# Splitting the first matmul of chunk 0 so that a part of it runs inside the attention that comes before it

## The chip, the cores and the metric

The kernel runs on one core of a Trainium2 chip. The metric is the device time of one execution in microseconds; the median over several executions is quoted, and a trace of one execution shows where the time goes. Every trace counts from its own first instruction, and where that zero lies differs from trace to trace by about 1 us. So intervals inside one trace are compared here, and absolute times only with that in mind.

## The reference, cut to what matters

```python
# q, k, v: (8 rows, 8 heads, 576 positions, 64)
# heads 0..3: sliding window of 32; heads 4..7: every fourth position of a window of 128
attn = softmax(mask(q @ k.T / 8)) @ v                # per row and head
x = attn.transpose(0, 2, 1, 3).reshape(8 * 576, 512) # 4608 tokens
h = x @ w_in                                         # 512 -> 2048  ("mm1")
g = relu(h) ** 2
out = g @ w_out                                      # 2048 -> 512  ("mm2")
```

The 4608 tokens go through mm1 and mm2 in nine chunks of 512. Chunk 0 is the first 512 of row 0's 576 tokens, so it needs all of row 0's attention; its mm2 runs interleaved with the attention of row 1.

## The kernel before: the parts that matter

One ff tile of mm1 is four matmuls (one for each 128 of the 512 features) into a PSUM bank, then a relu on ScalarE and, for each pair of tiles, a square on VectorE:

```python
def mm1_gen(c, g, sm=None):
    xs = xT[:, :, c * TOKC : (c + 1) * TOKC]
    for ffc in range(NFF):                           # 16 ff tiles
        ph = pmool.tile([P, TOKC], FP32, ...)
        for n, dmk in enumerate((2, 3, 0, 1)):
            nc.tensor.matmul(ph, wi[:, dmk, ffc * P : ffc * P + P], xs[:, dmk, :], ...)
            if n == 1:
                yield
        relu_squared(c, ffc, g, ph, rts)
        yield
```

`pump(n)` takes n steps of the pending generator, which is how matmuls are laid between other work. The end of row 0's attention, the loads for row 1, and chunk 0:

```python
    zs = av_dilated(0, 1, 0)
    s_sliding_half(1, 1)
    x_dilated(0, 0, ys, False)
    idle(4)                                  # zero matmuls: keep TensorE's clock up
    zs += av_dilated(0, 1, 1)
    xs += av_sliding(0, 3, 5)
    xs += av_sliding(0, 5, 6, nc.scalar)
    constants_late()
    idle(16)
    x_dilated(0, 1, zs, False)               # transposes, then a ScalarE copy into xT
    idle(16)
    x_sliding(0, 1, xs, False)
    idle(12)

    load_w_out(0, 1)                         # GpSimd's queue
    landed(wi[:, NDM - 1, 1023:1024])        # GpSimd waits for w_in's second quarter
    nc.gpsimd.memset(sq[:, :, :, 0:1], 0.0)
    load_sliding_qk(1)                       # sq: row 1's sliding q and k (SyncE's queue)
    load_dilated_qk(1)                       # nd_: row 1's dilated q and k
    load_w_out(1, 2)
    landed(nd_[:, 0, 1, 12 * D - 1 :])
    ...                                      # memsets
    load_v(1)
    landed(sv[:, NB - 1, HH - 1, D - 1 :])
    load_w_out(2, 4)
    dk = keep_qk(2)

    g0 = hidden(0)
    pending.append(mm1_gen(0, g0))
    pump(28)                                 # 14 of 16 tiles
    cast_sliding_qk(1, (nc.scalar, nc.vector, nc.scalar, nc.vector))   # reads sq
    pump(1000)
    pending.append(mm2_by_rows_gen(0, g0))
    pump(1)
    for hp in range(2):
        for i in (1, 0):
            t_sliding(1, hp, i, True)        # transposes of the casts
            pump(1)                          # two matmuls of mm2
    ...
```

The softmax here doesn't subtract the row's maximum and nothing guards it: scores larger than these inputs give would overflow.

## Time and profile before

| | |
|---|---|
| time, first three executions | 306.88 us median (306.87 to 307.14) |
| TensorE busy | 296.3 of 305.5 us |
| zero matmuls in the second half of row 0's attention (16.9 to 25.0 us) | 60 |
| chunk 0's mm1, undivided | 13.97 us, from 24.96 to 38.93 (13.81 of it, from 25.12, on the chain that ends last) |
| first transposes of row 1 | 39.21 us |
| chunk 1's mm1 starts | 63.25 us |

How to read it: TensorE is the resource, but "busy" counts zeros too. The lines that carry this are in the prediction and not shown again. A granted clock of 1.00 means TensorE at full speed. Names in the lines: ph and po are the PSUM tiles of mm1 and mm2, rt is a tile after the relu, sq holds row 1's sliding q and k as loaded, early their casts to 16 bits, pt the transposes of those and QKTp the copy of pt.

### The profile page before, as it was taken

The numbers are of one execution on the slowest core, as the hardware profiler recorded it, in microseconds if no ns is written. First come the engines' busy times: TensorE is split into PE (matmuls) and PEld (weight loads), VectorE is DVE, ScalarE is ACT, GpSimd is POOL, SyncE is SP. The second block draws the span as 40 slices with busy tenths as digits, with TensorE's granted clock in tenths as the row PEclk, the third lists the DMA queues.
The fourth block names the chain that finished last, engine by engine and source line by source line (L and its number), as shares of the span: only waits on it lengthen the run. The fifth ranks groups of instructions, "written<-read, shape, count | busy, mean of one in ns | idle before, by whom it ended". The sixth has DMA issues, their size and how long they took to land.

```text
span 305.5 us, 7013 instructions
## 1 busy us (share of the span) xinstructions
PE 296.3 (97%) x2898; PEld 192.8 (63%) x2898; DVE 208.8 (68%) x410; ACT 185.0 (61%) x308; POOL 48.5 (16%) x97
## 2 busy tenths in 40 slices
PE   8899998999999999999999999999999999999994
PEld 3675444444696469646964697459745974684584
DVE  4653475849966797679766977697769775843744
ACT  6466777478834893489348943894389437405610
POOL 7454013006004100320032003200100010000000
PEclk9999999999999999999999999999999999999999
DMA  8999989899899998689939983989310012003004
GB/s 175 226 213 230 233 174 203 160 232 269 210 191 219 310 170 185 217 182 198 228 111 197 216 184 123 213 184 209 117 72 0 2 61 78 2 0 137 2 0 138
DMA packets 85615, 47.89 MB, mean 157 GB/s; under 512 B 68112, under 2 KB 82896, under 8 KB 85200
## 3 DMA queue, kind: packets, MB, share of 16 engines
q1 hardware_dynamic: 76688, 27.24, 40.8%
q0 software_dynamic: 8352, 19.80, 28.9%
q8 instruction: 22, 0.36, 0.5%
q10 hardware_dynamic: 544, 0.43, 0.5%
q14 instruction: 9, 0.07, 0.1%
HBM read 39.85 MB, written 16.52 MB: 184 GB/s over the span
## 4 chain that ended last, share of the span: by engine, by line
PE 90%; ACT 3%; DMA 3%; POOL 2%; issue 1%; DVE 1%; ACTq 0%; POOLq 0%
PE ph L388 42%; PE pob L438 9%; PE poa L438 9%; PE poe L438 5%; PE poc L438 5%; PE pod L438 4%; PE po L409 4%; DMA early<-in_q_dram 3%; PE paw L776 3%; PE pav L759 2%; PE pz L675 2%; PE ps L656 1%; PE py L809 1%; PE px L791 1%; POOL early L119 1%; ACT AT L628 1%
## 5 line engine op out<-in xcount | busy, mean ns | idle before, releaser
L388 PE MATMUL ph<-xT,wi 128*128 128x512 f16 x576 | 129.8, 379 | 0.0
L354 ACT ACTIVATE rt<-ph 128x512 f16<-128x512 f32 x144 | 84.9, 601 | 36.4 <-PE ph L388 36.1
L388 PEld LDWEIGHTS <-wi 128*128 128x128 f16 x576 | 54.4, 98 | 62.4
L358 DVE TENSOR_TENSOR g<-rt 128x1024 f16<-128x1024 f16 x63 | 43.5, 691 | 47.2 <-ACT rt L354 47.0
L438 PEld LDWEIGHTS <-sm 128*128 128x128 f16 x512 | 46.9, 98 | 4.8
L438 PEld LDWEIGHTS <-g 128*128 128x128 f16 x384 | 35.9, 98 | 6.9 <-DVE g L356 1.3
L438 PE MATMUL pob<-T,sm 128*128 128x256 f16 x256 | 32.5, 272 | 0.0
L438 PE MATMUL poa<-wo,g 128*128 128x256 f16 x256 | 32.4, 273 | 0.0
L458 POOL DMA_DIRECT2D out_dram<-otl x6 | 4.6, 763 | 152.6 <-DVE otl L493 152.6
L815 ACT COPY xT<-py 128x576 f16<-128x576 f16 x16 | 10.2, 640 | 27.3 <-PE py L809 27.3
L740 DVE TENSOR_TENSOR x_d<-paw,rcp_d 72x512 f16<-72x512 f32 x32 | 22.0, 687 | 1.1
L797 ACT COPY xT<-px 128x576 f16<-128x576 f16 x16 | 10.3, 642 | 13.6 <-PE px L791 13.6
L409 PE MATMUL po<-wo,g 128*128 128x512 f16 x64 | 17.8, 379 | 0.0
L735 DVE RECIPROCAL rcp_d<-paw 72x8 f32<-72x8 f32 x32 | 6.4, 199 | 16.2 <-PE paw L776 16.2
L628 ACT ACTIVATE AT<-pz 128x576 f16<-128x576 f32 x28 | 16.6, 652 | 1.0 <-PE pz L675 0.6
L628 ACT ACTIVATE AT<-ps 128x576 f16<-128x576 f32 x28 | 16.6, 649 | 0.5
L740 DVE TENSOR_TENSOR x_p<-pav,rcp_p 96x512 f16<-96x512 f32 (+1 forms) x24 | 16.2, 676 | 0.8
L438 PE MATMUL poe<-wo,sm 128*128 128x256 f16 x128 | 16.3, 273 | 0.0
L438 PE MATMUL pod<-T,g 128*128 128x256 f16 x128 | 16.3, 272 | 0.0
L438 PE MATMUL poc<-T,sm 128*128 128x256 f16 x128 | 16.2, 272 | 0.0
L478 ACT COPY otu<-poa 128x512 f32<-128x512 f32 x8 | 4.7, 586 | 17.5 <-PE poa L438 17.5
L629 DVE TENSOR_TENSOR AT<-AT,maskd 128x576 f16<-128x576 f16 x28 | 12.2, 455 | 3.5 <-ACT AT L628 2.5
(120 smaller groups left out, 354.5 us busy)
## 6 DMA issues: line engine op xcount, KB each, us to landing
sv<-in_v_dram SPq DMA_DIRECT2D x40, 128.0 KB, 3.1
sd<-in_v_dram SPq DMA_DIRECT2D x8, 512.0 KB, 6.2
dk<-in_k_dram POOLq DMA_DIRECT2D x12, 288.0 KB, 7.0
dk<-in_q_dram POOLq DMA_DIRECT2D x12, 288.0 KB, 7.5
out_dram<-otl POOLq DMA_DIRECT2D x6, 512.0 KB, 3.3
out_dram<-otu POOLq DMA_DIRECT2D x6, 512.0 KB, 4.2
sd<-in_v_dram SPq DMA_DIRECT2D x8, 288.0 KB
wi<-in_moe_w_in_dram POOLq DMA_DIRECT2D x4, 512.0 KB, 10.3
```

The source lines that it names most:

```text
L354: nc.scalar.activation(rt[:, o, :], ph[:], ACTF.Relu)
L358: nc.vector.tensor_mul(g[:, ffc - 1 : ffc + 1, :], rt, rt)
L388: nc.tensor.matmul(ph, wi[:, dmk, ffc * P : ffc * P + P], xs[:, dmk, :], start=(n == 0), stop=(n == NDM - 1),)
L409: nc.tensor.matmul(po, g[:, ffc, t * P : (t + 1) * P], wo[:, ffc, :], start=(ffc == 0), stop=(ffc == NFF - 1),)
L438: nc.tensor.matmul(acc, lhs[:, k, t * P : (t + 1) * P], rhs[:, k, :], start=(first and k == 0), stop=(k == NK - 1), skip_group_check=True,)
L628: nc.scalar.activation(AT[:, u, 0:UW], ps[:, :, 0 : UW // 2], ACTF.Exp, scale=scale)
L629: nc.vector.tensor_mul(AT[:, u, 0:UW], AT[:, u, 0:UW], mask)
L735: nc.vector.reciprocal(rcp[0:w, 0:n], pv[:, :, :, D])
L740: nc.vector.tensor_tensor(out=x[0:w, 0:n], in0=pv[:, :, :, 0:D], in1=rcp[0:w, 0:n].unsqueeze(3).to_broadcast([w, n, HH, D]), op=ALU.mult,)
L776: nc.tensor.matmul(pav[:, e, h * (D + 2) : h * (D + 2) + D + 1], AT[:, u, off : off + P], vd[:, t, 2 * a + e, h, 0 : D + 1], start=True, s ...
L797: nc.scalar.copy(xT[:, 0:2, t0 : t0 + 288], px[:, 0:UW].rearrange("x (c t) -> x c t", c=2),)
L815: nc.scalar.copy(xT[:, 2:4, t0 : t0 + 288].rearrange("x c (i r) -> x c i r", r=DIL), py[:, 0:UW].rearrange("x (c r i) -> x c i r", c=2, r= ...
```

## The change

The intent: tokens 0 to 287 of chunk 0 are ready while the second half of the attention still runs. The first eight ff tiles of those tokens go where the zero matmuls were; later the same eight tiles do tokens 288 to 511, and the other eight tiles run undivided. Cut to its core (the generator's new arguments and the helper `square_all`, which runs the squares that were put off, are left out):

```diff
     s_sliding_half(1, 1)
-    x_dilated(0, 0, ys, False)          # moved ahead of s_sliding_half(0, 1)
-    idle(4)
+    g0 = hidden(0)
+    squares: list = []
+    pending.append(mm1_part_gen(0, g0, 0, 288, 0, 8, squares))
+    pump(2)
     zs += av_dilated(0, 1, 1)
     xs += av_sliding(0, 3, 5)
-    xs += av_sliding(0, 5, 6, nc.scalar)
-    constants_late()
-    idle(16)
+    xs += av_sliding(0, 5, 6)
+    pump(2)
     x_dilated(0, 1, zs, False)
-    idle(16)
+    pump(2)
     x_sliding(0, 1, xs, False)
-    idle(12)
+    pump(1000)
+    square_all(squares)
+    constants_late()
 ...
-    pending.append(mm1_gen(0, g0))
-    pump(28)
+    pending.append(mm1_part_gen(0, g0, 288, TOKC, 0, 8, squares))
+    for _ in range(4):
+        pump(2)
+        square_all(squares)
+    pending.append(mm1_gen(0, g0, None, 8))
+    pump(13)
     cast_sliding_qk(1, (nc.scalar, nc.vector, nc.scalar, nc.vector))
```

Row 0's copies into xT are also cut in two, one for each 128 features.

## The prediction

> **What bounds the kernel now.** I read the page first, then the busy time by stretch, the chain of waits, and last the timeline and the transfers of the stretches that the change touches.
>
> ```profile
> span 305.5 us, 7013 instructions
> ...
> PE 296.3 (97%) x2898; PEld 192.8 (63%) x2898; DVE 208.8 (68%) x410; ACT 185.0 (61%) x308; POOL 48.5 (16%) x97
> ```
>
> TensorE is occupied almost throughout, so the kernel shortens if TensorE work leaves the path, or if padding is replaced by work. The stretches show where padding lies.
>
> ```profile
> 16.90:24.96 8.06, 7.51 (x144) 6.22 (x141) 4.07 (x11) 5.05 (x12) 3.65 (x7) 1.00 1.24 206
> 24.96:38.93 13.97, 13.97 (x68) 6.37 (x66) 5.20 (x8) 9.71 (x17) 2.74 (x8) 1.00 1.12 226
> 38.93:52.66 13.73, 12.23 (x146) 6.55 (x144) 8.61 (x18) 10.38 (x19) 3.88 (x7) 1.00 0.97 187
> ...
> 94.98:305.49 210.51, 206.60 (x1934) 138.33 (x1931) 147.93 (x273) 122.67 (x201) 21.56 (x44) 1.00 0.56 133
> ```
>
> Columns: stretch, length, busy time of TensorE, weight loads, VectorE, ScalarE, GpSimd, then granted clock, DMA share, GB/s. The first row is the second half of row 0's attention, the second is mm1 of chunk 0, the third is row 1's attention interleaved with chunk 0's second matmul. Note the DMA share near 1 in the first three: that part runs beside a saturated load stream. From 95 us on TensorE is full and DMA is not, so any time won before 63 us should carry to the end unless a load stops it.
>
> TensorE looks full in the first row, but much of that is warm-up matmuls on zeros (pj):
>
> ```profile
> 21.64 1.05 PE L538 MATMUL pj<-zz 128*128 128x128 f16 x16
> 22.53 0.42 PE L809 MATMUL py<-ident,x_d 72*128 72x72 f16 x8
> 22.79 1.06 PE L538 MATMUL pj<-zz 128*128 128x128 f16 x16
> ```
>
> mm1 then stands whole on the chain that ends last (start, length, what):
>
> ```profile
> 25.12 13.81 PE ph L388 x64
> 38.94 0.43 PE po L409 x2
> 39.37 0.42 PE pt L563 x6
> ```
>
> So the intent is sound: work goes where zeros were multiplied. The question is what stops the earlier TensorE afterwards. The timeline just behind mm1 (start, length, engine, line, operation) and the transfers there decide it:
>
> ```profile
> 37.88 1.56 ACT L166 CAST early<-sq 96x768 f16<-96x768 f32 x2
> 37.88 0.69 DVE L358 TENSOR_TENSOR g<-rt 128x1024 f16<-128x1024 f16 x1 [1.03 <-ACT rt L354]
> 38.49 1.80 DVE L168 CAST early<-sq 96x768 f16<-96x768 f32 x2
> ...
> 39.35 1.07 ACT L354 ACTIVATE rt<-ph 128x512 f16<-128x512 f32 x2
> ...
> 40.69 0.64 ACT L166 COPY QKTp<-pt 128x576 f16<-128x576 f16 x1 [0.27 <-PE pt L563]
> ...
> 41.38 0.41 PE L563 MATMUL pt<-ident,early 96*128 96x96 f16 x6 [0.29 <-ACT QKTp L166]
> ```
>
> The casts of row 1's q and k (sq) start as soon as ScalarE and VectorE reach them, without a shown wait. But the transfers of sq are barely in. Of its queue, the transfer view of 37.30 to 37.39 us still has one packet (the line below: queue, packets, MB, share), and the view of 37.4 to 38.5 has none; the packet starts at 37.36. So sq lands at about 37.4, only 0.45 us before its cast.
>
> ```profile
> q1 hardware_dynamic: 1, 0.00, 1.5%
> ```
>
> The other landings that matter, each one issue and its us to landing: the first two quarters of w_in (issued 12.71 and 13.49, so 21.0 and 23.6), and the third quarter of w_out (issued 44.99, so 51.2).
>
> ```profile
> wi<-in_moe_w_in_dram POOLq DMA_DIRECT2D x1, 512.0 KB, 8.3
> wi<-in_moe_w_in_dram POOLq DMA_DIRECT2D x1, 512.0 KB, 10.1
> wo<-in_moe_w_out_dram POOLq DMA_DIRECT2D x1, 512.0 KB, 6.2
> ```
>
> **What the Trainium skill says.** "TensorE: Matmul & The Clock Gate", section "Wait — 56ns, not 53.3ns?": a warm matmul follows the last after N / 2.4 GHz plus about 2.5 ns. The trace agrees: 13.81 us / 64 = 215.8 ns at 512 columns. For 288 and 224 columns, which no matmul train here has, I take 122.5 and 95.8 ns as estimates from that section. The same page, "What's actually happening", says that the clock falls after an idle window of some 3.4 us; the trace shows a granted clock of 1.00 in all rows, and the gaps I expect without the zeros are under 1 us, so I expect no loss there. "ScalarE: Activation LUTs", "What ACT_TABLE_LOAD costs": an ACTIVATE with immediate operands takes 186 ns + 0.833 ns per element, and neighbours overlap by 93 ns. For 288 that gives 426 ns; the trace's 128x288 copies took 402 ns, two in 0.70 us. I use about 0.40 for 288 and 0.37 for 224. "DMA: Bandwidth & Descriptors", "Why a DMA increments its semaphore by 16 and not by 1": the engines of a transfer finish independently, and only all 16 increments mean that it has landed. The trace fits: 68 packets of the sq queue start between 35 and 36 us, six between 36 and 37, and the last, a 4-byte one, at 37.36.
>
> **The change part by part.** *Removed:* 48 zero matmuls (4+16+16+12) at about 55.8 ns = 2.7 us, and 32 full matmuls, 32 x 215.8 = 6.91 us, from the whole block of mm1. *Added in the gaps:* eight tiles x four matmuls x 122.5 = 3.92 us. *Added afterwards:* 32 x 95.8 = 3.07 us. So the block behind the attention falls from 13.81 to 3.07 + 6.91 = 9.98 us, 3.83 less, while the gap region grows.
>
> When does the block start? Today at 24.96. In the new order: the transposes of the first dilated half come earlier (0.25 us), so the last scores end near 20.8; tiles 0 and 1 wait for w_in until 21.1 and end at 22.1; the values (20 matmuls, 0.71 us today) end at 22.8; tiles 2 and 3 at 23.8; eight transposes at 24.0. VectorE, with three normalisations from 22.5 at a pitch of 0.85, finishes at 24.8. (The last moves from ScalarE, where its four pieces took 0.92, to VectorE; today's like piece took 0.42.) If tile 4 takes the PSUM buffer of that last normalisation it waits until 24.9; I choose this. Tiles 4 and 5 to 25.9, transposes to 26.1, tiles 6 and 7 to 27.0. The copies of xT, two of 0.40 pitched 0.30, are done at 27.1, just when their matmuls need them. Block from 27.0, end at 37.0 against 38.8: **1.8 us earlier** on TensorE. Without the buffer wait it would be 2.6.
>
> The eight new relus at 0.40 fit between; deferred squares (four of about 0.46, from 0.69 at 1024 and 0.42 at 512 elements) run on an idle VectorE. Both are off the path.
>
> *What is kept of the 1.8.* Row 1's casts stand after tile 13 in program order. Tile 13's relu would now end at 36.1, but sq lands at 37.4; its loads were issued at 23.9 and 24.4, behind w_in's second landing, which the change does not touch. So the casts start at about 37.45: 0.43 earlier on ScalarE, 1.04 on VectorE (38.49 today, since a square stood before them). From there both chains run at today's lengths. VectorE's q cast ends at 39.25, transposes by 39.6. ScalarE's casts are followed by the last two relus, 37.45 + (40.42 - 37.88) = 39.99, and then by the copy QKTp, which had waited 0.27 for TensorE and now waits no more: 39.9 against 40.69, **0.8 earlier**. The transposes at 41.38 wait for that copy and shift by the same. Behind them TensorE and ScalarE alternate as today. The third quarter of w_out, in at 51.2 and used at 52.66, allows 1.4, so it does not bite. Row 2's transposed q and k (landed at 65.9, used at 70.7) leave room too. Sum: 1.8 won, about 1.0 given back at the sq wait, 0.8 left: 306.88 - 0.8 = **306.1 us**.
>
> **The rivals.** (a) The saving passes whole, 1.8 to 2.6: 304.3 to 305.1. For it speaks that the casts show no wait today; against it the packet at 37.36, and w_out at 51.2, which would cap it at 1.4 anyway (305.4). (b) ScalarE alone sets the pace after the wait: 0.43 kept, 306.4. For it: relus 14 and 15 stand behind the casts; against it the 0.27 slack before the copy. (c) The gap region swells: w_in's second quarter at 23.6, the buffer wait, or ScalarE's longer queue of split copies and relus move the block's start beyond 28.1; then the win is under 0.8 and, if the start slips to 28.9, gone: 306.9. Against it: the stalls I could find add up to 27.0. (d) The clock falls without the zero matmuls; every gap is too short for that, and it would cost well over 1 us: 308 or more.
>
> **Range and chances.** The sq wait makes the result insensitive to my error in the gap region: any block start before 28.0 gives about the same. What moves it is the landing of sq's slowest engine, perhaps 0.3 us either way, and which of (b) or VectorE's 1.04 holds. Range 305.5 to 306.6. Faster by 2% needs 6.1 us, more than the 3.92 us moved; slower by 2% needs a fallen clock or a stall of six us that I cannot see. So 0.01, 0.98, 0.01.
>
> **What would show it.** In the changed profile: 32 matmuls of 288 columns between 21 and 27.1, then the block's end at about 37; tiles 0 and 1 waiting for w_in near 21.0; a wait of ScalarE or VectorE of over 1 us for the transfer of sq, ending near 37.4; QKTp's first copy near 39.9; the first use of w_out's third quarter near 51.9 without a wait; all later stretches as long as today. If sq lands before 36.5, or no wait for it appears, my main step is wrong and the saving is nearer 1.4. If the block starts after 28, the gap arithmetic is wrong.

## The result, and the profile after

The changed kernel took 307.10 us in the median of four executions (306.56 to 307.71); the kernel before, with one more execution beside them, 306.88 (306.63 to 307.14). The ratio was 1.0008, with a 95% interval of 0.9987 to 1.0029: no gain. (A ratio here is the mean time of one kernel's runs over that of the other's of the same rounds, so not quite the ratio of the medians.) Executions over 1.5% slower than the fastest of the same kernel are left out of the means.

The work did move. In the stretches of the changed kernel, cut at the same times as those of before (columns as there):

```profile
16.90:24.96 8.06, 7.17 (x110) 5.42 (x108) 4.09 (x10) 5.63 (x14) 3.72 (x8) 1.00 1.24 206
24.96:38.93 13.97, 12.01 (x88) 7.54 (x86) 6.88 (x16) 9.35 (x22) 2.62 (x7) 1.00 1.12 226
38.93:52.66 13.73, 12.52 (x131) 6.46 (x128) 7.68 (x17) 9.93 (x19) 3.92 (x8) 0.88 0.95 185
...
94.98:305.49 210.51, 206.89 (x1936) 138.56 (x1934) 148.16 (x274) 122.88 (x202) 21.54 (x44) 1.00 0.57 134
```

The second row has a hole: TensorE is busy for 12.01 of 13.97 us, where it was busy throughout. The third row shows something that I had ruled out: a mean granted clock of 0.88, where it was 1.00. The last row is nearly as before. It can't show by itself that nothing was won or lost there, since both were cut at the same times; but from the start of chunk 1's mm1 to the last matmul it took 238.33 or 238.34 us in all sixteen traces of this document. What the change does to the matmuls is decided before chunk 1. (From the last matmul to the end of the trace it is 3.6 us in the changed kernel and its variants, 3.8 to 4.0 in the kernel before and its two.)

TensorE's timeline around the end of mm1 in the changed kernel (start, length, instruction, idle time before it and what ended that):

```profile
35.83 0.38 PE L393 MATMUL ph<-xT,wi 128*128 128x512 f16 x1
36.04 0.59 PE L414 MATMUL po<-wo,g 128*128 128x512 f16 x2
38.60 0.43 PE L568 MATMUL pt<-ident,early 96*128 96x96 f16 x6 [1.97 <-ACT early L166]
38.87 0.96 PE L414 MATMUL po<-wo,g 128*128 128x512 f16 x2
39.62 0.68 PE L568 MATMUL pt<-ident,early 96*128 96x96 f16 x6
40.10 1.05 PE L414 MATMUL po<-wo,g 128*128 128x512 f16 x2
```

The first pair of mm2 matmuls (po) stands at 36.04 instead of 38.78, so the block ends 2.74 us earlier. Then TensorE is idle for 1.97 us until row 1's casts (early) are there. After it, a pair of po matmuls takes 0.96 to 1.05 us, where the pair at 36.04 took 0.59. The granted clock explains that; here it is by short stretches (the three numbers that end a row are granted clock, DMA share and GB/s):

```profile
37.00:38.00 1.00, 0.00 (x0) 0.00 (x0) 0.34 (x1) 0.28 (x1) 0.00 (x0) 1.00 1.19 197
...
38.60:39.50 0.90, 0.90 (x8) 0.47 (x9) 0.87 (x2) 0.90 (x2) 0.28 (x3) 0.70 0.29 48
39.50:40.50 1.00, 1.00 (x8) 0.63 (x7) 0.64 (x2) 0.92 (x3) 0.00 (x0) 0.50 0.53 111
...
42.50:43.00 0.50, 0.50 (x9) 0.21 (x5) 0.00 (x0) 0.19 (x1) 0.00 (x0) 1.00 1.20 269
```

The clock is 1.00, then a mean of 0.70, then 0.50, then 1.00 again. The trace's clock record gives the half-speed stretch as 3.41 us, from 38.96 to 42.38.

And the casts wait for a load, as the chain of waits of the changed kernel says (start, length, what):

```profile
24.29 13.35 DMA sq<-in_k_dram
37.64 0.02 issue
...
37.72 0.84 ACT early L166
...
38.60 0.43 PE pt L568 x6
```

The load of row 1's k (sq) now sets the end of the stretch, from its issue at 24.29 to its landing at 37.64. In the trace of before, the record of completion increments has the sixteenth and last one of this load at 37.80, 0.07 us ahead of ScalarE's cast at 37.88. So the cast had no visible wait there because relu 13 ended at the same moment.

The sum: the first transposes came 0.61 us earlier (38.60 against 39.21). From there to the start of chunk 1's mm1 it took 24.93 us instead of 24.04, 0.89 longer. Chunk 1 therefore started 0.28 us later, and the rest is alike. Only the 0.89 is an interval inside each trace; the 0.61 and the 0.28 compare two zeros. Counted from the issue of sq's k instead (24.29 and 24.40), they are 0.50 earlier and 0.39 later.

### The profile page after: what moved, and what is told of

Same layout as the page of the kernel before. It is cut to its first block, busy times and chain, and to the rows that moved or that the text cites. A ratio compares the mean times of both kernels' runs of the same rounds, so it can differ in the third digit from the quotient of the medians.

```text
span 305.5 us, 6998 instructions
## 1 busy us (share of the span) xinstructions
PE 294.4 (96%) x2882; PEld 193.5 (63%) x2882; DVE 209.8 (69%) x415; ACT 185.3 (61%) x316; POOL 48.7 (16%) x97
## 4 chain that ended last, share of the span: by engine, by line
PE 86%; DMA 7%; ACT 3%; POOL 2%; issue 1%; DVE 0%; SPq 0%; ACTq 0%; POOLq 0%
PE ph L393 37%; PE pob L443 9%; PE poa L443 9%; PE poe L443 5%; PE poc L443 5%; DMA sq<-in_k_dram 4%; PE pod L443 4%; PE po L414 4%; DMA early<-in_q_dram 3%; PE paw L781 3%; PE pav L764 2%; PE pz L680 2%; PE ps L661 1%; PE py L816 1%; PE px L796 1%; POOL early L119 1%
## 5 line engine op out<-in xcount | busy, mean ns | idle before, releaser
L393 PE MATMUL ph<-xT,wi 128*128 128x512 f16 x544 | 122.9, 379 | 0.0
L354 ACT ACTIVATE rt<-ph 128x512 f16<-128x512 f32 x136 | 80.1, 601 | 34.0 <-PE ph L393 33.7
L393 PEld LDWEIGHTS <-wi 128*128 128x128 f16 x544 | 51.3, 98 | 58.6
L358 DVE TENSOR_TENSOR g<-rt 128x1024 f16<-128x1024 f16 x59 | 40.8, 691 | 41.0 <-ACT rt L354 40.7
L823 ACT COPY xT<-py 128x576 f16<-128x576 f16 (+1 forms) x18 | 10.4, 588 | 28.1 <-PE py L816 28.1
L414 PE MATMUL po<-wo,g 128*128 128x512 f16 x64 | 19.1, 401 | 0.0
L804 ACT COPY xT<-px 128x576 f16<-128x576 f16 (+1 forms) x18 | 10.4, 588 | 13.6 <-PE px L796 13.6
```

Of the source, the lines that this page charges most:

```text
L354: nc.scalar.activation(rt[:, o, :], ph[:], ACTF.Relu)
L358: nc.vector.tensor_mul(g[:, ffc - 1 : ffc + 1, :], rt, rt)
L414: nc.tensor.matmul(po, g[:, ffc, t * P : (t + 1) * P], wo[:, ffc, :], start=(ffc == 0), stop=(ffc == NFF - 1),)
L804: nc.scalar.copy(xT[:, c0:c1, t0 : t0 + 288], px[:, 288 * c0 : 288 * c1].rearrange("x (c t) -> x c t", t=288),)
L823: nc.scalar.copy(xT[:, 2 + c0 : 2 + c1, t0 : t0 + 288].rearrange("x c (i r) -> x c i r", r=DIL), py[:, 288 * c0 : 288 * c1].rearrange("x ( ...
```

## The experiments

**Theory A:** row 1's q and k (sq) land at about 37.7 us whatever TensorE does; the earlier block only makes TensorE wait for them, and that idle stretch halves its clock for one window, which takes back the little that was left. **Rivals.** B: the wait alone eats the gain, the clock is a bystander. C: the narrow matmuls and split copies cost what they save. D: the halved clock hides behind the other engines. E: a gain from easing the load stream would be the load stream's own, with the moved work worth nothing.

Each trace gave these times (us from that trace's start; "block end" is the start of the first mm2 pair, "landed" the last completion increment of sq's k):

| kernel | sq landed | block end | first transposes | chunk 1 starts | from the last but one to the last | half clock inside |
|---|---|---|---|---|---|---|
| before | 37.80 | 38.78 | 39.21 | 63.25 | 24.04 | no |
| changed | 37.64 | 36.04 | 38.60 | 63.53 | 24.93 | 3.41 |
| changed, again | 38.43 | 36.37 | 39.39 | 64.45 | 25.06 | 3.41 |
| four tiles | 37.73 | 37.58 | 38.70 | 62.80 | 24.10 | no |
| changed, half of sq | 32.28 | 35.66 | 36.09 | 60.13 | 24.04 | no |
| before, half of sq | 33.86 | 38.82 | 39.25 | 63.28 | 24.03 | no |
| padded, one tile | 37.64 | 36.19 | 38.61 | 63.31 | 24.70 | no |
| padded, two tiles | 37.37 | 35.87 | 38.33 | 63.02 | 24.69 | no |
| real fill | 37.17 | 35.75 | 38.13 | 62.56 | 24.43 | 3.41 |
| dilated loads held back | 35.06 | 36.12 | 36.55 | 68.29 | 31.74 | 10.24 |
| casts late | 36.90 | 35.56 | 37.87 | 61.81 | 23.94 | no |
| casts late, padded | 37.83 | 36.52 | 38.80 | 62.56 | 23.76 | no |
| sq early | 32.27 | 36.06 | 36.49 | 63.84 | 27.35 | 3.41 |
| sq and v early | 32.91 | 35.56 | 35.99 | 60.05 | 24.06 | no |
| before, sq and v early | 32.86 | 38.69 | 39.12 | 63.15 | 24.03 | no |
| four tiles, sq and v early | 31.93 | 37.40 | 37.83 | 61.86 | 24.03 | no |

**1. The changed kernel again, as a control.** No edit.

> The changed kernel once more, as the control for the other three. Theory A (the sq landing at 37.6 to 37.8 us holds both kernels, and in the changed one TensorE idles some 2.1 us before it, after which the clock is halved for one window of 3.4 us): ratio to before 0.999 to 1.003, granted clock 0.994 in most executions, and a half-clock stretch just behind the sq wait. Theory B (the idle TensorE costs nothing by itself, the whole gain is eaten by the sq wait alone): the same time; the clock dip would be a bystander.

Measured: 308.27 us median (305.69 to 310.07, six executions) against 306.92 of before; ratio 1.0039 (1.0007 to 1.0071). The change can be slower than nothing. The single executions, each with its own mean granted clock, sort themselves. Over this and the first round: clock 0.999 or 1.000: 306.56 and 305.69. Clock 0.994: 306.95, 307.25, 307.71, 307.99, 308.20, 308.34 and 308.54. Clock 0.988: 310.07. One window of 3.41 us at half speed in 305 us is 0.5 x 3.41 / 305 = 0.0056, so 0.994 fits one such window and 0.988 two (the execution at 0.988 was not traced). This is not yet a proof that the clock costs the time: a later load makes both the wait and the dip longer.

**2. Zero matmuls in the wait.**

```diff
     pending.append(mm2_by_rows_gen(0, g0))
     pump(1)
+    idle_matmuls(pa("pw")[:, 0, :], 32, P)
```

> 32 zero matmuls of 128 columns (about 1.8 us) after the first pair of the second matmul, so TensorE isn't idle while row 1's q and k land; nothing else changes. Theory A: granted clock back at 1.00 behind the wait, block of chunk 1 starts 0.4 to 0.8 us earlier than in the changed kernel, time 0.3 to 0.9 us under before (306.0 to 306.6), ratio 0.997 to 0.999. Theory B: no gain over the changed kernel, ratio 1.000 to 1.002.

Measured: 307.03 us (306.30 to 307.25), before 306.92, ratio 0.9997 (0.9983 to 1.0011). The clock stayed up (no half-speed stretch before the end of the trace), the gain did not come. The timeline of TensorE in this run shows why:

```profile
36.62 1.95 PE L543 MATMUL pw<-zz 128*128 128x128 f16 x32
38.61 0.43 PE L568 MATMUL pt<-ident,early 96*128 96x96 f16 x6
...
41.44 0.41 PE L568 MATMUL pt<-ident,early 96*128 96x96 f16 x6 [1.17 <-DVE QKTp L168]
```

The third set of transposes waits 1.17 us for a copy on VectorE. In the changed kernel the same transposes waited for ScalarE's copy; the PSUM buffer that they were given had become another. So this run changed two things, and its miss says nothing for B or against A.

**3. The same in two PSUM tiles of 16**, which I thought would keep the buffers in step.

```diff
+    for n in range(2):
+        idle_matmuls(pa(f"pw{n}")[:, 0, :], 16, P)
```

> As the run with 32 zero matmuls, but in two PSUM tiles of 16, so that the transposes behind them keep the buffers that they have in the changed kernel (with one tile the third transpose waited 1.17 us for VectorE's copy instead of 0.57 or less for ScalarE's). Theory A: clock 1.00, sq in near 37.7, third transpose near 40.9, chunk 1's block 0.4 to 0.6 us ahead of before: ratio 0.997 to 0.999 (306.0 to 306.6). Theory D (once sq is late the clock is not what costs): no faster than the changed kernel of the same rounds or than before, 1.000 or more.

Measured: 307.32 us (306.73 to 307.98), before 306.40, ratio 1.0021 (1.0006 to 1.0037). A miss: the instruction order shows the third transposes still waiting for VectorE, and the trace has the same 1.17 us. I take the reason to be that the buffers are handed out by an order of release that the program's builder assumes, and not by turns; no run tests that.

**4. Only four tiles moved.**

```diff
-    pending.append(mm1_part_gen(0, g0, 0, 288, 0, 8, squares))
+    pending.append(mm1_part_gen(0, g0, 0, 288, 0, 4, squares))
 ...     # likewise for tokens 288 to 511; the undivided part starts at tile 4
```

> Only four of the eight tiles go into the gaps, the other twelve stay whole. Theory A: the block ends about 1.8 us later than in the changed kernel, still before the landing of sq; TensorE idles well under 1 us, the clock stays up, and moving half as much gives MORE than moving all: 0.3 to 0.8 us under before, ratio 0.997 to 0.999. Theory B: the same as the changed kernel, 1.000 to 1.002. Theory C (the narrow 288 and 224 column matmuls or the split copies cost the gain): half the cost, so between the two, no idle involved.

Measured: 306.12 us (305.78 to 306.54), before 306.92, ratio 0.9975 (0.9962 to 0.9987). Half the move gives more than the whole, as theory A said and C did not. Its casts and first transposes:

```profile
37.76 1.81 DVE L168 CAST early<-sq 96x768 f16<-96x768 f32 x2 [0.38 <-DMA sq<-in_k_dram]
37.81 1.57 ACT L166 CAST early<-sq 96x768 f16<-96x768 f32 x2 [1.16 <-DMA sq<-in_k_dram]
...
38.70 0.43 PE L568 MATMUL pt<-ident,early 96*128 96x96 f16 x6 [0.52 <-ACT early L166]
```

The load lands when it landed in the changed kernel, 37.7; TensorE waits 0.52 us instead of 1.97, and the clock stays at 1.00. From the end of the block on, this kernel and the changed one have the same order on TensorE and the same dependencies. They enter that stretch within 0.1 us of each other (38.70 and 38.60), and it takes 24.10 us here and 24.93 there. That difference, 0.8 us, is the cleanest measure here of what the halved clock costs; it speaks against B and D. (Here TensorE waits 0.57 us for ScalarE's copy before the third transposes; in the changed kernel, which reaches them later, no such wait is left.)

**5. The wait taken away: half the load.**

```diff
-                out=sq[:, i, :, :],
-                in_=src[b, 0:HH].rearrange("h (p j) d -> p h (j d)", j=6),
+                out=sq[:, i, 0:2, :],
+                in_=src[b, 0:2].rearrange("h (p j) d -> p h (j d)", j=6),
```

> Wrong result on purpose: of row 1's sliding q and k only two of four heads are loaded, so sq lands some 3 us earlier; the casts and all else stay. Theory A: no wait for sq, no clock dip, the casts start right behind tile 13's relu near 35.3, and the 2.7 us by which the block ends earlier show up: 2 to 3 us under before (304 to 305), unless the third quarter of w_out (it also comes earlier here) or another load stops it. Theory B: the same. Theory C: still no faster than before.

Measured: 303.85 us (303.64 to 304.31), before 306.92, ratio 0.9903 (0.9888 to 0.9917). (The comparison with the reference passed at its tolerance all the same.) sq is in by 32.3, the first transposes start at 36.09, behind the block with no wait, and the stretch after them takes 24.04, exactly that of before.

**6. The same half load in the kernel before.**

> The kernel before, with the same half load of row 1's q and k (wrong result on purpose): what the early sq is worth without the moved work. Theory A: sq is in on time for TensorE there, so 0 to 0.3 us gained, ratio 0.999 to 1.000; then nearly all of the 3.07 us of the changed kernel with the half load is the moved work. Theory E (the half load itself is worth the 3 us, by freeing the load stream): about 304, ratio 0.990.

Measured: 306.61 us (306.43 to 307.20), before 306.40, ratio 0.9999 (0.9984 to 1.0014). The early load alone is worth nothing. E falls for this pair: the 3 us of run 5 are the moved work, let through.

**7. Real work in the wait**: casts behind the last relus, five pairs of mm2 before the first transposes, four pairs fewer later.

```diff
-    pump(13)
+    pump(1000)
     cast_sliding_qk(1, (nc.scalar, nc.vector, nc.scalar, nc.vector))
-    pump(1000)
     pending.append(mm2_by_rows_gen(0, g0))
-    pump(1)
+    pump(5)
 ...
-        pump(1 + g)
+        pump(g)
 ...
-    scores_dilated(1, lambda: pump(2))
+    scores_dilated(1, lambda: pump(1))
```

> The changed kernel with real work in the wait: row 1's casts stand behind the last relus, ten matmuls of the second product (five pairs, 2.2 us) run before the first transposes, and four pairs fewer between the later scores. Theory A: TensorE idles under 0.5 us before sq, clock 1.00; the later stretch has 1.7 us less matmul work on it; 0.8 to 1.5 us under before (305.4 to 306.1), capped by the third quarter of w_out near 51.2. If the later waits were covered only by those pairs, the gain shrinks to that of the zero matmuls, 306.0 to 306.6.

Measured: 306.47 us (305.72 to 308.52), before 306.40, ratio 1.0002 (0.9977 to 1.0026). A miss. Now the thinned stretch idles: the scores wait for ScalarE, and the third quarter of w_out stops TensorE after all:

```profile
48.92 0.31 PE L680 MATMUL pz<-QKTd 64*128 64x72 f16 x8 [1.08 <-ACT AT L633]
...
51.45 1.01 PE L414 MATMUL po<-wo,g 128*128 128x512 f16 x2 [0.28 <-DMA wo<-in_moe_w_out_dram]
```

The pair at 51.45 takes 1.01 us: the half clock has moved to this place (49.64 to 53.06). It came in four of six executions (0.992 or 0.994), which took 306.28 to 308.52; the other two took 306.14 and 305.72.

**8. The dilated loads held back** until w_out's first quarter is in.

```diff
+    landed(wo[:, 3, DM - 1 :])
     load_dilated_qk(1)
     load_w_out(1, 2)
```

> The changed kernel with the loads of row 1's dilated q and k issued only when the first quarter of w_out has landed, so that sq has the stream to itself at its end. Theory A: sq lands 1 to 1.8 us earlier (35.8 to 36.7), TensorE's idle stretch falls under 1 us, clock 1.00, casts near 36.5; the dilated loads land near 39.5 and push the third quarter of w_out to about 52, which takes some of it back: 0.4 to 1.2 us under before (305.7 to 306.5). If sq still lands after 37.4, the late engine isn't held up by those loads, and the time stays at 307.

Measured: 311.62 us (308.82 to 313.09), before 306.40, ratio 1.0144 (1.0105 to 1.0183). The half that I expected came: sq landed at 35.06 in this trace. But every later load came later too, which I had put at 1 us:

```profile
45.34 0.59 PE L414 MATMUL po<-wo,g 128*128 128x512 f16 x2 [2.04 <-DMA wo<-in_moe_w_out_dram]
...
55.73 1.01 PE L414 MATMUL po<-wo,g 128*128 128x512 f16 x2 [0.72 <-DMA wo<-in_moe_w_out_dram]
```

The second and third quarters of w_out landed 4.2 and 4.5 us later than in the changed kernel (45.30 against 41.07, 55.69 against 51.21), and 10.24 us of half clock fell into the stretch (51.23 to 61.47). The edit did more than intended: w_out's second quarter stands behind the dilated loads on the same queue, so the new wait held it back too, and it was issued at 37.27 instead of 26.54. The run shows what that cost, not what the dilated loads alone would have.

**9 and 10. Casts behind the last relus, without and with zero matmuls.** These two have the same order on TensorE but for the zeros.

```diff
-    pump(13)
+    pump(1000)
     cast_sliding_qk(1, (nc.scalar, nc.vector, nc.scalar, nc.vector))
-    pump(1000)
 # run 10 only, behind mm2's first pair, into a bank of mm2 not yet begun:
+    idle_matmuls(row_banks[1], 32, P)
```

> The changed kernel with row 1's casts behind the last two relus instead of ahead of them, no padding. Its order and its waits on TensorE are those of the next run but for the zero matmuls, so the two are the clean pair for the clock that the two earlier padded runs weren't (there the third transpose waited for VectorE's copy, which came late because relus 14 and 15 stood behind the casts). Theory A: relus 14 and 15 no longer wait for sq, the third transpose finds its buffer free, which wins some 0.4 to 0.6 us over the changed kernel; but TensorE idles 2 us and the clock halves: 306.3 to 307.0, ratio 0.998 to 1.002.

> The same with 32 zero matmuls (1.8 us) into a PSUM bank not yet in use, ahead of the first transposes. Theory A: clock 1.00, and 0.6 to 1.0 us faster than the run without them in the stretch from the first transpose to chunk 1; 305.4 to 306.2, ratio 0.995 to 0.998. Theory D (the halved clock hides behind the other engines): the two equal within 0.2 us.

Measured: run 9 took 306.53 us (305.05 to 307.79), ratio 0.9975 (0.9945 to 1.0006); run 10 took 306.40 (305.56 to 310.40, the last left out of the ratio), ratio 0.9991 (0.9947 to 1.0034); before 307.07 (306.54 to 308.23). As a comparison this is inconclusive. In its trace, run 9 idled and kept its clock all the same:

```profile
37.87 0.43 PE L568 MATMUL pt<-ident,early 96*128 96x96 f16 x6 [1.71 <-ACT early L166]
```

Its six executions are plainer: 305.05, 305.53 and 306.05 with clocks of 0.998 to 1.000, and 307.01, 307.45 and 307.79 with 0.994. With the padding, one of six still had 0.994 (310.40), and one took 309.50 with a clock of 1.000. No trace of those two executions was looked at, so what made them slow is not known; a very late load is my guess.

**11. sq issued earlier**: the same bytes, 3.5 us earlier, and a correct result.

```diff
     load_w_out(0, 1)
-    landed(wi[:, NDM - 1, 1023:1024])
     nc.gpsimd.memset(sq[:, :, :, 0:1], 0.0)
     load_sliding_qk(1)
+    landed(wi[:, NDM - 1, 1023:1024])
     load_dilated_qk(1)
```

> The changed kernel with row 1's sliding q and k issued 3.4 us earlier (before the wait for the second quarter of w_in, not after it); same bytes, right result. Theory A: sq lands near 35, at the price of w_in's third and fourth quarters and w_out's first, each up to 1.5 us later; TensorE's idle stretch before the transposes falls under 1 us and the clock stays: 0.5 to 1.4 us under before (305.0 to 305.9), capped by w_out's third quarter at 51.2. If the stream only shifts the wait to w_in's fourth or w_out's first quarter, 306 to 307.

Measured: 305.80 us (304.57 to 307.89), before 307.07, ratio 0.9965 (0.9931 to 0.9999). sq landed at 32.27 (I had expected some 35) and no longer stops anything; the next stop is the one that my prediction had computed as a cap:

```profile
51.88 1.01 PE L414 MATMUL po<-wo,g 128*128 128x512 f16 x2 [1.78 <-DMA wo<-in_moe_w_out_dram]
```

w_out's third quarter landed at 51.84, TensorE had waited 1.78 us for it, and a window of half clock followed (51.85 to 55.27). Four executions without it took 304.57 to 305.96, two with it (0.992) 307.55 and 307.89.

**12. The same, and v issued earlier.**

```diff
-    landed(nd_[:, 0, 1, 12 * D - 1 :])
+    landed(nd_[0:48, 1, 1, 12 * D - 1 :])
```

The load of v had waited for the last dilated q; it now waits for the first part of the dilated k. That closes a hole in the load stream between 38 and 40.5 us. The same stretch in the changed kernel and then in this one (the last two numbers are DMA share and GB/s):

```profile
38.00:40.50 2.50, 1.90 (x15) 1.10 (x16) 2.10 (x4) 2.42 (x5) 0.28 (x3) 0.69 0.41 77
```

```profile
38.00:40.50 2.50, 2.29 (x30) 1.26 (x29) 1.16 (x2) 1.27 (x3) 0.00 (x0) 1.00 1.21 246
```

> The same, and row 1's v issued once the first part of the dilated k has landed (36.2) rather than the last of q (38.5), which closes the gap in the load stream near 39 us, so w_out's third quarter lands near 49.5. Theory A: 1.2 to 2.2 us under before (304.2 to 305.2). If w_out's third quarter does not come earlier, the same as the run with early sq alone.

Measured: 304.09 us (303.40 to 306.58), before 307.07, ratio 0.9906 (0.9874 to 0.9938), result correct. w_out's third quarter landed at 49.56 and no wait is left in front of it. But its first use starts at 49.60, 0.04 us later: this load too is now a bound that shows no wait. The result beats both kernels, by 0.9% of the time of before.

**13. The kernel before with this load order.**

> The kernel before with the new load order alone (row 1's sliding q and k issued before the wait for w_in, v after the first part of the dilated k). Theory A: TensorE is on its path there with nothing to be had from earlier loads: 0 to 0.4 us gained, ratio 0.999 to 1.001. Theory E (the load order is worth the 3 us by itself): 303.5 to 305, ratio 0.990 to 0.994. A later w_in third and fourth quarter (27 and 31.5 us) could cost it up to 0.5.

Measured: 306.53 us (306.47 to 307.22), before 306.69, ratio 0.9997 (0.9985 to 1.0009). The load order by itself is worth nothing, the change by itself is worth nothing; together they are worth 2.9 us. E falls.

**14. Four tiles with this load order.**

> Four tiles moved instead of eight, with the new load order. Theory A: now the shorter move gives LESS: its block ends about 1.6 us later than with eight, and nothing waits in front of it, so 304.8 to 306.0 where eight tiles gave 304.1, ratio to before 0.994 to 0.997. If four are still as good as eight (303.8 to 304.4), something other than the sq wait made the difference before.

Measured: 305.65 us (305.42 to 307.44), before 306.69, ratio 0.9977 (0.9956 to 0.9998). With the old loads four tiles beat eight (0.9975 against 1.0039 in the same rounds). With the new ones eight beat four (0.9906 against 0.9977; these two ran in different rounds). The reversal turned round, as theory A requires. The ratio for four tiles is nearly the same under either order, and above the 0.994 to 0.997 that I expected. In the traces the new order did help them: the wait of 0.52 us is gone and chunk 1 starts at 61.86 instead of 62.80. One execution of six, 307.44 at a clock of 0.998, pulls the mean up; it was not traced, and what slowed it is not known.

## Why the prediction was wrong, point by point

- **The change's cost and the block.** Right in kind. The matmuls of 288 and 224 columns had the estimated pace: the 40 of both widths from 25.09 on span 4.21 us, where 8 x 0.1225 + 32 x 0.0958 = 4.05 plus the end of the last one is expected. The start of tile 4 was off: I chose a wait for a PSUM buffer until 24.9, and it started at 23.84 without one. The block ended at 36.04, not 37.0: 2.7 us earlier instead of 1.8, close to the 2.6 that I had named for the case without that wait.
- **"What is kept of the 1.8", the landing of sq.** The mechanism was right: the casts wait for sq, which lands when it did. The time was too early. I took the start of the load's last packet, 37.36, plus nothing to speak of for its landing, 37.4. The last completion increment was at 37.80, and 37.64 in the changed kernel, where the last packet had started at 37.00. So before there was no 0.45 us of room but 0.07.
- **The casts.** I predicted 0.43 us earlier on ScalarE and 1.04 on VectorE. Measured, 0.16 (37.72 against 37.88) and 0.83 (37.66 against 38.49). The first transposes were 0.61 earlier, and the copy QKTp on ScalarE started at 40.34 against 40.69, 0.35 earlier; I had said 0.8, where my own sum (39.99 against 40.69) gives 0.7.
- **The step that failed: "the gaps I expect without the zeros are under 1 us, so I expect no loss there", and with it rival (d), dismissed as "every gap is too short for that".** I looked for gaps only where the zeros had been. The long one is where the saving itself ends: TensorE earlier by 2.7 us in front of a load that is not. It idled 1.97 us, and a window of 3.41 us at half clock followed. Against the four-tile kernel, alike from there on, that cost 0.8 us. So 0.61 kept at the transposes, minus 0.89 in the stretch behind them, is 0.28 us lost where 0.8 were promised.
- **Rival (d)'s size.** I gave a fallen clock "well over 1 us: 308 or more". The first four executions gave 306.56 to 307.71, the control a median of 308.27.
- **Rival (a)'s cap.** Right, and seen in run 11: once sq is early, w_out's third quarter at 51.8 stops TensorE.
- **The range.** In the executions that kept a clock of 0.999 or more, 306.56 and 305.69, the predicted 306.1 holds; they are two of ten. I also took the insensitivity to the block's start for safety. It meant the reverse: each microsecond gained in front of the load becomes idle time.

What stays open: what exactly drops the clock. It is not the length of one pause: a half-speed stretch followed on waits of 1.97 and 2.43 us before the first transposes, on one of 1.78 in run 11, and in run 7 on a window whose longest wait was 1.08; after one of 1.71 in run 9 the clock stayed. The clock records say more. In all sixteen traces, the stretches of one clock last whole multiples of 3.413 us (10, 1 and 77 of them in the changed kernel, 13, 3 and 73 in run 8; the last one is cut off by the end), so the clock changes at the edges of windows of that length. What can then count is how busy TensorE was inside a window. Of all the windows that began at full clock, by the matmul records of the traces, every one with less than 1.54 us of matmuls was followed by half speed (1.45 in the changed kernel, from 35.55 to 38.96; 0.98 in the control; 1.53 in run 11), and none with more than 1.98. In between, two were (1.71 in run 8, 1.98 in run 7) and four were not (one of them 1.76, in run 9), so busy time alone gives no sharp limit. The edges lie differently in each trace (the changed kernel's first full-speed stretch starts at 4.83 us in one and at 6.12 in the other), which may be why some executions escape; that is not shown, since those were not traced.

The clean pair for the clock (runs 9 and 10) was inconclusive, so its cost rests on the four-tile comparison and on how single executions sort by their clock. The landing of sq differs between executions (36.9 to 38.4 in the traces that load all of it at its old place, with the other loads unmoved) mostly because its issue does: it was issued at 23.77 to 25.19 us and landed 12.9 to 13.4 us later in all nine of these traces.

## What to carry to other kernels

A load that lands just as its reader happens to become free shows no wait and is nevertheless a bound: before you make an engine earlier, list the landing of every load that its next stretches need, by completion and not by the last packet, and compare it with the new time of use. If an earlier TensorE meets a load that isn't earlier, the gain becomes an idle stretch, and the idle stretch can cost more than it should through the clock; then move less, or move the load first. A change and a reordering of loads can each be worth nothing alone and nearly 1% together, so a flat result is no reason to drop a change whose saving can be seen stopped by one wait.

## What the Trainium skill lacked or had wrong

- "TensorE: Matmul & The Clock Gate", "What's actually happening", gives the idle condition as one whole window of some 3.4 us, and "HAM oscillation — how this bites in real kernels" puts it as no idle gaps above some 3.4 us. Here the window before the drop was not idle: TensorE was busy for 1.45 of its 3.41 us, the idle stretch in it was 1.97 us, and the half-speed stretch began 0.36 us after TensorE had resumed. In run 7 a window with 1.98 us busy and no wait above 1.08 was enough. (A later section there, "A second HAM failure mode: psum-queue depth-cycling", has a clock that swings with short idles, but gives no length.) What agrees is the length of the window, 3.41 us, and that its edges don't follow the kernel. Those two sections would mislead whoever allows gaps of 2 us.
- "DMA: Bandwidth & Descriptors", "Why a DMA increments its semaphore by 16 and not by 1", says that the engines of a transfer finish independently, but not by how much they differ. In the trace of before, fifteen of the sixteen increments of sq's k lay between 36.05 and 36.98 us and the last at 37.80: one engine held the load up by 0.8 us. That last increment came 0.44 us behind the start of the load's last packet (0.64 in the changed kernel), which is what I had left out.
- "TensorE: Matmul & The Clock Gate" lists the total throttled time as a metric of a profile; no page says that the mean granted clock of an execution counts these windows (0.994 for one in 305 us), which is the quickest way to see from a list of times which executions had one. A half-speed stretch behind the last matmul lowers it as well, to 0.998 in the traces of runs 4 and 9, or to 0.992 together with one window in run 11, and costs no matmul anything.
